# The last three expert weights loaded by column halves, and new step orders around them

## The chip, the cores and the metric

The kernel runs on one core of a Trainium2 chip. The metric is the device time of one execution in microseconds (us); lower is better. Times are medians of several executions, and the profile is one execution more.

## What is computed

Block-sparse attention feeds a soft mixture of experts. The reference, cut to what matters here:

```python
# attention: q, k, v are (4, 8, 768, 64); chunks of 32 keys, the best 6 chunks of each query are kept
ub = np.sum(np.maximum(q * k_min, q * k_max), axis=-1)          # bound of a chunk, causal
sel = the 6 chunks of largest ub;  mask = sel & causal
attn = softmax(where(mask, q @ k.T / 8, -1e9));  x = attn @ v   # then reshaped to (3072, 512)
# experts: phi (512, 32), w1 (8, 512, 1024), w2 (8, 1024, 512); 8 experts with 4 slots each
logits = x @ phi
d = softmax(logits, axis=0);  slot_input = d.T @ x              # over all 3072 rows
for e in range(8):
    slot_out[e] = relu(slot_input[e] @ w1[e]) @ w2[e]
c = softmax(logits, axis=1);  out = c @ slot_out                # (3072, 512), f32
```

All inputs and the output are float32 in DRAM. The kernel computes in bfloat16 with float32 sums.

## The kernel before

**Attention.** The 4 x 8 heads are taken as 16 pairs (0 to 15). An outer loop runs over i from -2 to 16, and in each round a string in the table `ORDER` (or `PLAIN`) names the steps to issue, one after the other. Every engine gets its instructions in that order, so the strings are the schedule: an engine that waits for one step holds up all that stands behind it in its own queue. Round i issues the scores (S0 to S5), the exponentials on ScalarE (E0 to E5) and the causal edges on GpSimd (A0 to A5) of pair i, the product with v of pair i-1 (P0 to P5), the bounds and the search for pair i+1 (UB, SL, SH, UN, NT, NC), the transposes of k and q for pair i+2 (KT, KE, KN, KX, QT, QE, QP, BD), and the normalising of pair i-2 (NO, XT, XE). Loads are steps too: LK, LQ, LV, W.

**The chain behind attention.** Rounds 13 to 15 also hold the expert softmax of the first three batches (MX, MT, MB, MS, MD, ME and RM, RS, RE). Round 16 is the chain behind the last pair: the last pair's product with v (ZPA, ZP3, ZP4, ZP5), normalising (ZN0, ZN1, ZN2), transposes and their copies (ZX0 to ZX2; Ze on ScalarE, ZE on VectorE), logits (ZL1, ZL3, ZL4), the maximum and its spreading (ZPM, ZPT, ZMB, ZLK, ZL2, ZSH, ZBC), the exponential (ZDX), the old batches' share of the slot inputs (D0 to D4, 18 matmuls each; DA copies the sum), the last batch's share (ZD0, ZD1), the sums (ZSA, ZS0, ZS1, ZSZ). Zk is a dummy matmul of 128 columns. Then the experts: `I{f}{g}` is the first product for hidden half f and expert group g, R0 and R1 the relu of half f, T0 and T1 the transposes of its result, `O{f}{g}{y}` the second product for output-column half y, O0 and O1 the slot outputs of half y.

**Output.** `H{m}.{y}` writes column half y of row group m (256 KB), `F{m}` a whole row group (512 KB). There are 12 groups; the first six are written by halves, all six left halves (y = 0) ahead of O011, O111 and O1, so ahead of any right half. The stores go through SyncE's queue.

**Weights.** All 16 weight matrices stay in SBUF as `w_sb[0..15]`: 0 to 7 are w1 and 8 to 15 are w2. Each is 2 MB in DRAM and is cast to 1 MB on the way by a DMA that GpSimd issues. Weights 0 to 11 have memory of their own. The last four take memory that attention gives up: number 12 in step CL (behind the last k and q), 13 in CU (behind the last bounds), 14 in ZCT (behind the last transposed k and q), 15 in ZCE (behind the last exponentials). `load_w` loads numbers 14 and 15 by column halves: the left half when the memory comes free, and both right halves in `close_e`, between the memory sets of two padded tiles (`siT`, `hT`) and of `zrow`. A half is two DMAs of 256 KB, one for each hidden half. The left half feeds the y = 0 products, the right half the y = 1 products.

Of the kernel before, what the change touches and what calls it, by code (L numbers as in the profile page):

```python
# [39 lines left out]
for _g, _pieces in enumerate(GROUPS):  # L40
# [11 lines left out]
LV A4 QP A5 BD""",  # L52
    1: """LV KT S0 LQ S1 LK UB E0 S2 E1 NO S3 P0 P1 A0 P2 SL KE SH E2 QT P3 A1 XT UN XE S4 W S5 KN E3 QE E4 E5
A5 P4 A2 KX A3 NT LG BD A4 NC P5 LC QP""",
    13: """S0 KT LV E0 S1 UB E1 A1 KE NO S2 S3 E2 E3 P0 P1 SL UN QT SH P2 QE P3 A3 A2 KN KX XT S4 S5 CL XE QP
E4 A0 W BD E5 P4 NT A5 LG P5 NC A4 LC MX""",
    14: """S0 E0 S1 UB S2 NO MT S3 RM P0 E1 E2 P1 E3 MB SL A1 A2 MS S4 MD A0 SH E4 UN P2 RS S5 XT P3 P4 A3 NT
NC E5 XE RE CU A4 A5 P5""",
    15: """NO S0 S1 C0 E0 S2 E1 P0 S3 E2 E3 V0 A1 XT P1 P2 A3 S4 A0 S5 P3 E4 A4 A2 E5 ME A5 P4 P5 XE""",
    16: """ZN0 ZPA ZP3 ZCT ZP4 D0 ZLH ZX0 ZN1 ZP5 Ze0 ZN2 D1 ZX1 ZL1 ZX2 D2 Ze1 ZL3 ZE2 ZL4 ZPM Zk ZPT ZMB D3  # L60
ZLK ZL2 ZSH ZBC D4 Zk ZCE ZDM ZDX DA ZD0 ZCI ZDE Zk ZSA ZS0 ZD1 ZS1 I00 I10 I01 I11 R0 ZRM R1 ZSZ
ZLC T0 C1 O000 V1 ZZ T1 O010 O100 O110 ZCX Zk Q0 O0 H0.0 O001 H1.0 Q1 H2.0 O101 H3.0 H4.0 H5.0 O011
O111 O1 H0.1 C2 V2 H1.1 Q2 F6 H2.1 F7 C3 v3 H3.1 F8 Q3 H4.1 F9 F10 H5.1 F11""",
}

# [2 lines left out]
def kernel(  # L68
# [16 lines left out]
    E, F = moe_w1.shape[0], moe_w1.shape[2]  # L85
# [4 lines left out]
    NO = OLD * NQT  # L90
# [50 lines left out]
    def load_w(i, ys=range(2)):  # L141

        if i < E:
            src = moe_w1[i].rearrange("(a p x) f -> p a (x f)", p=P, x=2)
            dst = w_sb[i].rearrange("p (a f) -> p a f", a=NDG // 2)
        else:
            src = moe_w2[i - E].rearrange("(a p x) d -> p a (x d)", p=P, x=4)
            dst = w_sb[i].rearrange("p (a f) -> p a f", a=NFG // 4)
        if i >= 2 * E - 2:
            src = moe_w2[i - E].rearrange("(a p x) (y d) -> y a p x d", p=P, x=4, y=2)  # L150
            dst = w_sb[i].rearrange("p (a x y d) -> y a p x d", a=NFG // 4, x=4, y=2)
            for y in ys:
                for a in range(2):
                    nc.gpsimd.dma_start(out=dst[y, a], in_=src[y, a])  # L154
        else:
            nc.gpsimd.dma_start(out=dst, in_=src)  # L156
# [41 lines left out]
    for n in "I K1 Q1 K2 Q2 W G M".split():  # L198
        if n[0] == "I":
            make_identity(nc, ident)  # L200
        elif n[0] == "W":
            load_w(0)
        elif n[0] == "V":
            load_v(int(n[1]))
        elif n == "G":
            nc.gpsimd.affine_select(
                out=qgrp, in_=qgrp, compare_op=ALU.not_equal, fill=1.0, base=0,
                pattern=[[-1, 4], [0, CH]], channel_multiplier=1,
            )
            nc.gpsimd.affine_select(  # L210
                out=caus[:4], in_=caus[:4], compare_op=ALU.is_ge, fill=NEG, base=0,
                pattern=[[0, 4], [-1, 4]], channel_multiplier=1,
            )
        elif n == "M":
            nc.gpsimd.affine_select(
                out=squad, in_=squad, compare_op=ALU.not_equal, fill=-NEG, base=0,
                pattern=[[-CH, 2], [-64, 2], [-1, NCHUNK]], channel_multiplier=1,
            )
            nc.gpsimd.affine_select(
                out=squad, in_=squad, compare_op=ALU.not_equal, fill=1.0, base=-NCHUNK,  # L220
                pattern=[[-CH, 2], [-64, 2], [0, NCHUNK]], channel_multiplier=1,
            )
        else:
            load(int(n[1]), n[0].lower())
# [319 lines left out]
    def weights(i):  # L544
        nonlocal nw
        for _ in range(wplan.get(i, 0)):
            load_w(nw)
            nw += 1

    def late_weight(*ys):  # L550
        n = len(w_sb)
        wt = ctx.enter_context(tc.tile_pool(name=f"wt{n}", bufs=1))
        w_sb.append(wt.tile([P, NFG * Dm], BF16, name=f"w_sb{n}"))
        load_w(n, *ys)
# [15 lines left out]

    def close_bounds(i):
        u_ctx.close()
        late_weight()

    def of(d, f, *a):
        return lambda i: f(i + d, *a) if have(i + d) else None
# [7 lines left out]
        "NO": of(-2, normalise), "XT": of(-2, x_transposes), "XE": of(-2, evac_x),  # L584
        "LG": lambda i: moe(moe_logits, i - 2), "LC": lambda i: moe(moe_copy, i - 2),
        "PHI": phi_load, "kc": lambda i: cast_first("k"), "qc": lambda i: cast_first("q"), "MASK": spread_mask, "CL": close_loads, "CU": close_bounds,
    }
    for g in range(len(GROUPS)):
# [23 lines left out]
    def close_e():  # L612
        e_ctx.close()
        late_weight([0])
        pads = ctx.enter_context(tc.tile_pool(name="pads", bufs=1))
        st["siT"] = pads.tile([P, NDG, E, CH], BF16, name="siT_pad")
        st["hT"] = pads.tile([P, NFG, E, CH], BF16, name="hT_pad")
        nc.gpsimd.memset(st["siT"], 0.0)
        load_w(2 * E - 2, [1])
        nc.gpsimd.memset(st["hT"], 0.0)  # L620
        st["tail"] = ctx.enter_context(tc.tile_pool(name="tail", bufs=1))
        st["zrow"] = st["tail"].tile([1, 4, CH], F32, name="zrow")
        nc.gpsimd.memset(st["zrow"], 1.0)
        load_w(2 * E - 1, [1])
# [94 lines left out]
    def slots_z():  # L719
# [8 lines left out]
    HX = range(NDG - 1)  # L728
    STEP.update({n: (lambda i, f=f, a=a: f(*a)) for n, f, *a in (
        ("ZCT", close_T), ("ZCE", close_e), ("ZCI", close_i), ("ZN0", normalise, LAST - 1),  # L730
        ("ZPA", pv, LAST, [0, 1, 2]), ("ZP3", pv, LAST, [3]), ("ZP4", pv, LAST, [4]), ("ZP5", pv, LAST, [5]),
        ("ZX0", x_transposes, LAST - 1), ("ZE0", evac_x, LAST - 1, 0, NQT, nc.vector.tensor_copy),
# [174 lines left out]
```

## Time and profile before

| | |
|---|---|
| median of 3 runs | 157.3 us (157.18 to 157.82) |
| the profiled execution's own time | 157.73 us |
| its span, first to last instruction | 155.8 us, mean granted TensorE clock 0.964 |
| busy: TensorE, VectorE, ScalarE, GpSimd | 87%, 75%, 79%, 63% of the span |
| read from DRAM, written to DRAM | 52.49 MB, 6.29 MB |

The profile gives busy time by engine and by stretch of time, the DMA engines' busy share and what they moved (counted on the SBUF side for a load, so a cast load of 200 GB/s reads 400 GB/s), groups of instructions by code line with what they waited for, and a chain of waits followed back from the last instruction. A busy share of the DMA engines above 1 means that more than one packet per engine was under way.

### The profile page before, as it was taken

The numbers are of one execution on the slowest core, as the hardware profiler recorded it, in microseconds if no ns is written. First come the engines' busy times: TensorE is split into PE (matmuls) and PEld (weight loads), VectorE is DVE, ScalarE is ACT, GpSimd is POOL, SyncE is SP. The second block draws the span as 40 slices with busy tenths as digits, with TensorE's granted clock in tenths as the row PEclk, the third lists the DMA queues.
The fourth block names the chain that finished last, engine by engine and source line by source line (L and its number), as shares of the span: only waits on it lengthen the run. The fifth ranks groups of instructions, "written<-read, shape, count | busy, mean of one in ns | idle before, by whom it ended". The sixth has DMA issues, their size and how long they took to land.

```text
span 155.8 us, 6234 instructions
## 1 busy us (share of the span) xinstructions
PE 135.7 (87%) x2591; PEld 95.5 (61%) x2591; DVE 117.0 (75%) x408; ACT 123.5 (79%) x165; POOL 98.3 (63%) x196
## 2 busy tenths in 40 slices
PE   6649899998999999999999999998999999877700
PEld 3335467766776777676767766685759856545400
DVE  5766979988889889898888989899946343439900
ACT  3669999999899999999989999998796303447900
POOL 7959895977789687796977885855627970000000
PEclk9956999999999999999999999999999999999995
DMA  4999999999999999999999999999999999998995
GB/s 161 176 207 199 168 220 183 193 216 186 213 194 206 201 184 212 196 208 200 182 208 200 207 202 200 207 203 192 200 215 211 214 198 194 159 325 306 392 404 219
DMA packets 46251, 33.32 MB, mean 214 GB/s; under 512 B 26512, under 2 KB 41872, under 8 KB 46224
## 3 DMA queue, kind: packets, MB, share of 16 engines
q0 software_dynamic: 41552, 25.86, 115.1%
q1 hardware_dynamic: 4672, 7.08, 12.4%
q8 instruction: 20, 0.33, 0.8%
q14 instruction: 7, 0.06, 0.1%
HBM read 52.49 MB, written 6.29 MB: 377 GB/s over the span
## 4 chain that ended last, share of the span: by engine, by line
POOL 26%; PE 20%; ACT 16%; DMA 14%; issue 10%; DVE 9%; POOLq 0%; ACTq 0%; DVEq 0%
ACT e_sb L365 10%; POOL e_sb L370 9%; DMA w_sb<-in_moe_w_dram 7%; DMA k_in<-in_k_dram 7%; POOL v_t L180 4%; PE at_ps L399 3%; PE sc_ps L342 3%; POOL q_in L163 3%; POOL w_sb L156 3%; POOL k_in L163 3%; ACT kT L249 2%; PE sc_ps L352 2%; PE tr_ps L240 2%; PE warm_ps L230 2%; POOL w_sb L154 2%
## 5 line engine op out<-in xcount | busy, mean ns | idle before, releaser
L365 ACT ACTIVATE e_sb<-sc_ps 128x768 bf16<-128x768 f32 (+1 forms) x96 | 83.0, 925 | 3.3 <-PE sc_ps L352 2.1
L370 POOL TENSOR_SCALAR_AFFINE_SELECT e_sb<-e_sb 128x256 bf16<-128x256 bf16 x96 | 37.1, 409 | 24.4 <-ACT e_sb L365 22.2
L342 PE MATMUL sc_ps<-qT,kT 64*128 64x384 bf16 (+3 forms) x288 | 39.9, 295 | 1.0 <-ACT e_sb L365 0.6
L352 PE MATMUL sc_ps<-nsT,smask 64*128 64x384 bf16 (+2 forms) x320 | 39.4, 278 | 0.0
L399 PE MATMUL at_ps<-v_t,e_sb 128*128 128x65 bf16 x672 | 27.7, 194 | 0.0
L399 PEld LDWEIGHTS <-e_sb 128*128 128x128 bf16 x672 | 23.9, 98 | 5.8 <-issue 5.3
L342 PEld LDWEIGHTS <-kT 64*128 64x128 bf16 x288 | 16.0, 94 | 10.0 <-issue 4.4
L352 PEld LDWEIGHTS <-smask 64*128 64x128 bf16 x320 | 17.4, 95 | 3.7 <-issue 0.4
L180 POOL DMA_DIRECT2D v_t<-in_v_dram x16 | 16.5, 1034 | 0.0
L412 DVE TENSOR_TENSOR x_sb<-at_ps,inv 128x768 bf16<-128x768 f32 (+1 forms) x17 | 15.5, 910 | 0.6
L259 DVE TENSOR_REDUCE mm<-kT 128x24 bf16<-128x768 bf16 x16 | 15.1, 943 | 0.1
L264 DVE TENSOR_REDUCE mm<-kT 128x24 bf16<-128x768 bf16 x16 | 15.1, 943 | 0.0
L249 ACT ACTIVATE qT<-tr_ps 128x768 bf16<-128x768 bf16 x16 | 13.0, 815 | 2.1 <-PE tr_ps L240 2.0
L307 DVE MAX8 mx_t<-ub_ps 128x8 f32<-128x16 f32 (+4 forms) x160 | 14.4, 163 | 0.0
L249 ACT ACTIVATE kT<-tr_ps 128x768 bf16<-128x768 bf16 x16 | 12.9, 805 | 0.7 <-PE tr_ps L240 0.7
L163 POOL DMA_DIRECT2D k_in<-in_k_dram x15 | 10.9, 726 | 0.8 <-issue 0.5
L163 POOL DMA_DIRECT2D q_in<-in_q_dram x15 | 10.8, 717 | 0.2 <-issue 0.2
L432 DVE COPY xT_sb<-xT_ps 128x768 bf16<-128x768 bf16 (+1 forms) x15 | 8.1, 543 | 2.8 <-PE xT_ps L421 1.6
L156 POOL DMA_DIRECT2D w_sb<-in_moe_w_dram x14 | 10.1, 718 | 0.0
L240 PE MATMUL tr_ps<-ident,k_in 128*64 128x128 bf16 x192 | 8.7, 229 | 1.5 <-DMA k_in<-in_k_dram 1.3
L240 PEld LDWEIGHTS <-k_in 128*64 128x64 bf16 x192 | 6.1, 113 | 5.9 <-DMA k_in<-in_k_dram 3.2
L240 PE MATMUL tr_ps<-ident,q_in 128*64 128x128 bf16 x192 | 9.0, 229 | 0.6 <-DVE q_in L174 0.4
(129 smaller groups left out, 215.3 us busy)
## 6 DMA issues: line engine op xcount, KB each, us to landing
w_sb<-in_moe_w_dram POOLq DMA_DIRECT2D x14, 1024.0 KB, 12.2
v_t<-in_v_dram POOLq DMA_DIRECT2D x16, 192.0 KB, 11.2
out_dram<-o_sb SPq DMA_DIRECT2D x12, 256.0 KB, 4.0
out_dram<-w_sb SPq DMA_DIRECT2D x6, 512.0 KB, 4.2
k_in<-in_k_dram POOLq DMA_DIRECT2D x15, 192.0 KB, 9.1
q_in<-in_q_dram POOLq DMA_DIRECT2D x15, 192.0 KB, 9.1
w_sb<-in_moe_w_dram POOLq DMA_DIRECT2D x8, 256.0 KB, 11.3
cT_all<-in_k_dram SPq DMA_DIRECT2D x1, 384.0 KB, 3.1
```

Source lines behind the costliest of these rows:

```text
L163: nc.gpsimd.dma_start(out=t, in_=src.rearrange("h (p g) d -> p h (g d)", p=P))
L180: nc.gpsimd.dma_start(out=v_t[i % NV][:, :, :, :D], in_=v[b, 2 * j:2 * j + 2].rearrange("h (g p) d -> p h g d", p=P),)
L240: nc.tensor.matmul(ps[h * 64:(h + 1) * 64, g, :], lhsT=src[:, h, g * D:(g + 1) * D], rhs=ident, is_transpose=True,)
L249: nc.scalar.activation(t.rearrange("d (p g) -> d p g", g=NQT), st.pop((nm + "ps", i)).rearrange("d g p -> d p g"), func=ACT.Copy, scale=-1 ...
L259: nc.vector.tensor_reduce(mm[:, 0, 0, :], kT, axis=AX.X, op=ALU.min, negate=True)
L264: nc.vector.tensor_reduce(st["mm", i][:, 1, 0, :], kT, axis=AX.X, op=ALU.max)
L342: nc.tensor.matmul(ps[:, h, c:c + w], lhsT=kT[r, kg * P:(kg + 1) * P], rhs=qT[r, qs], start=True, stop=False,)
L352: nc.tensor.matmul(ps[:, h, c + (f - t0) * P:c + (l - t0) * P], lhsT=smask[r, x, kg].rearrange("p a b -> p (a b)"), rhs=nsT[r, (f - x * NJ ...
L365: nc.scalar.activation(e[:, :, :w], st.pop(("scps", i, g))[:, :, :w], func=ACT.Exp, scale=-scale)
L370: nc.gpsimd.affine_select(out=e[:, :, :P], in_=e[:, :, :P], compare_op=ALU.is_ge, fill=0.0, base=0, pattern=[[0, 2], [1, P]], channel_mult ...
L399: nc.tensor.matmul(o, lhsT=st["e", i, g][:, h, c:c + P], rhs=v_t[i % NV][:, h, kg, :], start=(kg == 0), stop=(kg == t),)
L412: nc.vector.tensor_tensor(st["x", b][:, t0:t1, 2 * j:2 * j + 2, :].rearrange("p t h d -> p h t d"), at[:, :, :, :D], inv.broadcast_to([P, ...
```

## The change

Three things. Weight 13 joins 14 and 15 in being loaded by column halves: its left half is issued in CU, its right half in `close_e` ahead of the right half of 14. The strings for rounds 13, 14 and 15 are in a new order, with the same steps but two: the copy V0 moves from round 15 into round 16, and the exponential ME from round 15 into round 14. The string of round 16 is new too, up to O110; behind that it is as before. The order of the six left half groups and of all row groups behind them is the same in both kernels.

```diff
-    13: S0 KT LV E0 S1 UB E1 A1 KE NO S2 S3 E2 E3 P0 P1 SL UN QT SH P2 QE P3 A3 A2 KN KX XT S4 S5 CL XE QP
-        E4 A0 W BD E5 P4 NT A5 LG P5 NC A4 LC MX
+    13: S0 E0 S1 KT UB KE E1 LV S2 A1 QT E2 NO S3 P0 P1 SL CL QE KN P2 P3 E3 P4 UN KX P5 XT S4 XE A2 SH W S5
+        E4 E5 NT A3 LG QP A5 A0 NC A4 LC BD MX
-    14: S0 E0 S1 UB S2 NO MT S3 RM P0 E1 E2 P1 E3 MB SL A1 A2 MS S4 MD A0 SH E4 UN P2 RS S5 XT P3 P4 A3 NT
-        NC E5 XE RE CU A4 A5 P5
+    14: S0 E0 S1 S2 UB NO MT E1 MB S3 P0 P1 A0 E2 SL A1 P2 RM A2 E3 MS SH S4 S5 P3 E4 MD UN P4 A4 E5 P5 A3
+        NT RS ME XT A5 NC XE CU RE
-    15: NO S0 S1 C0 E0 S2 E1 P0 S3 E2 E3 V0 A1 XT P1 P2 A3 S4 A0 S5 P3 E4 A4 A2 E5 ME A5 P4 P5 XE
+    15: S0 S1 C0 NO S2 P0 E0 E1 P1 E2 XT S3 S4 A2 E3 A0 A3 P2 P3 E4 P4 A1 XE S5 P5 E5 A4 A5
-    16: ZN0 ZPA ZP3 ZCT ZP4 D0 ZLH ZX0 ZN1 ZP5 Ze0 ZN2 D1 ZX1 ZL1 ZX2 D2 Ze1 ZL3 ZE2 ZL4 ZPM Zk ZPT ZMB D3
-        ZLK ZL2 ZSH ZBC D4 Zk ZCE ZDM ZDX DA ZD0 ZCI ZDE Zk ZSA ZS0 ZD1 ZS1 I00 I10 I01 I11 R0 ZRM R1 ZSZ
-        ZLC T0 C1 O000 V1 ZZ T1 O010 O100 O110 ZCX Zk Q0 O0 H0.0 ...
+    16: D0 ZPA ZP3 Zk V0 ZN0 ZP4 ZX0 ZLH Ze0 ZN1 ZP5 ZN2 ZCT D1 ZX1 ZL1 ZX2 D2 ZE1 ZE2 ZL3 ZL4 D3 ZPM ZLK
+        ZPT ZMB ZL2 ZSH ZBC ZDM ZCE D4 ZDX DA ZCI ZD0 ZDE ZSA ZS0 ZD1 ZS1 I00 I01 I10 R0 ZRM I11 R1 ZSZ T0
+        C1 O000 V1 ZZ T1 O010 O100 O110 ZLC ZCX Zk Q0 O0 H0.0 ...

 def load_w(i, ys=range(2)):
-        if i >= 2 * E - 2:
+        if i >= 2 * E - 3:

 def close_bounds(i):
         u_ctx.close()
-        late_weight()
+        late_weight([0])

 def close_e():
         nc.gpsimd.memset(st["siT"], 0.0)
+        load_w(2 * E - 3, [1])
         load_w(2 * E - 2, [1])
         nc.gpsimd.memset(st["hT"], 0.0)
```

More of the change, by code (lines that the diff above doesn't have):

```diff
@@ L54 @@
 A5 P4 A2 KX A3 NT LG BD A4 NC P5 LC QP""",
[L55 to L60, printed above, removed]
-ZLK ZL2 ZSH ZBC D4 Zk ZCE ZDM ZDX DA ZD0 ZCI ZDE Zk ZSA ZS0 ZD1 ZS1 I00 I10 I01 I11 R0 ZRM R1 ZSZ
-ZLC T0 C1 O000 V1 ZZ T1 O010 O100 O110 ZCX Zk Q0 O0 H0.0 O001 H1.0 Q1 H2.0 O101 H3.0 H4.0 H5.0 O011
+    13: """S0 E0 S1 KT UB KE E1 LV S2 A1 QT E2 NO S3 P0 P1 SL CL QE KN P2 P3 E3 P4 UN KX P5 XT S4 XE A2 SH W S5
+E4 E5 NT A3 LG QP A5 A0 NC A4 LC BD MX""",
+    14: """S0 E0 S1 S2 UB NO MT E1 MB S3 P0 P1 A0 E2 SL A1 P2 RM A2 E3 MS SH S4 S5 P3 E4 MD UN P4 A4 E5 P5 A3
+NT RS ME XT A5 NC XE CU RE""",
+    15: """S0 S1 C0 NO S2 P0 E0 E1 P1 E2 XT S3 S4 A2 E3 A0 A3 P2 P3 E4 P4 A1 XE S5 P5 E5 A4 A5""",
+    16: """D0 ZPA ZP3 Zk V0 ZN0 ZP4 ZX0 ZLH Ze0 ZN1 ZP5 ZN2 ZCT D1 ZX1 ZL1 ZX2 D2 ZE1 ZE2 ZL3 ZL4 D3 ZPM ZLK
+ZPT ZMB ZL2 ZSH ZBC ZDM ZCE D4 ZDX DA ZCI ZD0 ZDE ZSA ZS0 ZD1 ZS1 I00 I01 I10 R0 ZRM I11 R1 ZSZ T0
+C1 O000 V1 ZZ T1 O010 O100 O110 ZLC ZCX Zk Q0 O0 H0.0 O001 H1.0 Q1 H2.0 O101 H3.0 H4.0 H5.0 O011
 O111 O1 H0.1 C2 V2 H1.1 Q2 F6 H2.1 F7 C3 v3 H3.1 F8 Q3 H4.1 F9 F10 H5.1 F11""",
```

## The prediction, made before the change was run

> **What bounds the kernel now.** I read the page first: the engine shares, the DMA row, the queues and the bytes.
>
> ```profile
> span 155.8 us, 6234 instructions
> DMA  4999999999999999999999999999999999998995
> GB/s 161 176 207 199 168 220 183 193 216 186 213 194 206 201 184 212 196 208 200 182 208 200 207 202 200 207 203 192 200 215 211 214 198 194 159 325 306 392 404 219
> HBM read 52.49 MB, written 6.29 MB: 377 GB/s over the span
> ```
>
> No compute engine is above 87%, but the DMA engines are at nine tenths or more from the second slice to nearly the end. For 34 slices they load (about 200 GB/s on the SBUF side, so 400 read), then they store at about 400. A reordering of compute can gain only where that stream has a hole or where its tail is badly used. So next came the chain of waits over the last third, in order of time (start, length, what), and the DMA rows by issue (the lines on landing stand under the issue that they belong to):
>
> ```profile
> 127.74 10.80 DMA w_sb<-in_moe_w_dram
> 138.58 0.61 PE so_ps L810 x13
> 139.22 0.48 ACT so_sb L817
> 139.74 0.28 PE o_ps L840
> 140.05 0.48 DVE o_sb L847
> ```
> ```profile
> L156 POOL DMA_DIRECT2D w_sb<-in_moe_w_dram x1: 716/716/716, 104.9 to 104.9; - x1
> DMA to landing us min/median/max: 17.2/17.2/17.2
> ```
> ```profile
> L156 POOL DMA_DIRECT2D w_sb<-in_moe_w_dram x1: 722/722/722, 110.7 to 110.7; - x1
> DMA to landing us min/median/max: 16.7/16.7/16.7
> ```
> ```profile
> L154 POOL DMA_DIRECT2D w_sb<-in_moe_w_dram x2: 742/742/742, 120.4 to 121.2; - x2
> DMA to landing us min/median/max: 11.3/11.6/11.9
> ```
> ```profile
> L853 SPq DMA_DIRECT2D out_dram<-o_sb x1: 612/612/612, 135.2 to 135.2; - x1
> ```
> ```profile
> L853 SPq DMA_DIRECT2D out_dram<-o_sb x1: 534/534/534, 140.7 to 140.7; - x1
> ```
>
> Weight 11 lands at 104.9 + 17.2 = 122.1, weight 13 (whole) at 110.7 + 16.7 = 127.4, the left half of 15 at 121.2 + 11.9 = 133.1, the last right half at 127.74 + 10.80 = 138.54. From a landing to the first store of that half it is 135.2 - 133.1 = 2.1 us on the left and 140.7 - 138.54 = 2.2 us on the right. Then the stretches of one microsecond (length; busy time of PE, PEld, DVE, ACT, POOL with instructions; clock, DMA share, GB/s), and the two DMA queues from 136.0 to 136.5 and from 136.5 to 137.0 (packets, MB, share); q0 holds the loads, q1 the stores:
>
> ```profile
> 133.00:134.00 1.00, 0.89 (x20) 0.61 (x20) 0.00 (x0) 0.28 (x1) 0.00 (x0) 1.00 1.44 195
> 135.00:136.00 1.00, 1.00 (x26) 0.67 (x22) 0.61 (x4) 0.60 (x3) 0.00 (x0) 1.00 0.89 114
> 141.00:142.00 1.00, 0.89 (x13) 0.83 (x14) 0.90 (x4) 0.28 (x2) 0.00 (x0) 1.00 0.47 164
> 150.00:151.00 1.00, 0.00 (x0) 0.00 (x0) 0.00 (x0) 0.00 (x0) 0.00 (x0) 1.00 1.04 422
> ```
> ```profile
> q0 software_dynamic: 94, 0.05, 69.5%
> q1 hardware_dynamic: 4, 0.00, 2.4%
> ```
> ```profile
> q1 hardware_dynamic: 101, 0.10, 61.0%
> q0 software_dynamic: 78, 0.04, 57.0%
> ```
>
> Three things are to be seen. **One:** the load stream falls from 195 to 114 GB/s before the stores move (4 packets before 136.5, 101 in the half microsecond behind it, so they begin 1.3 us behind their first issue). The drop says that some of the 16 DMA engines have finished all loads near 134.5 to 135 and others drag on. Landing needs the slowest. **Two:** from 136.5 stores and remaining loads share the slow engines, 101 packets against 78. **Three:** the left stores run out, and from 141 to 142 the share is 0.47; the right half's stores then fill the engines to the end, which compute no longer touches (150 to 151: no engine busy, share 1.04). So the end is set by the landing of the last right half: 2.2 us of compute, then 18 units of 256 KB (six right halves, six whole groups at two each), and the span ends 155.8 - 140.7 = 15.1 us behind the first right store's issue. Whatever moves the landing moves the end by as much.
>
> **The change part by part.** The sum is made on the profiled execution: 157.73 us, span 155.8, so 1.9 us lie around the span. It is 0.4 us over the median of 157.3; I carry the difference over to the median.
>
> *Weight 13 by halves, bytes.* The same 2 MB are read, in shorter pieces. Four DMAs of halves, the left of 14 and 15, landed between 127.4 and 133.1: 5.6 us per MB written; the whole weight 13 took 127.4 - 122.1 = 5.4. By rate it is more:
>
> ```profile
> 114.00:118.00 4.00, 3.87 (x84) 2.94 (x83) 0.89 (x3) 3.95 (x6) 2.09 (x6) 1.00 1.06 214
> 127.00:134.00 7.00, 6.70 (x135) 4.12 (x128) 1.30 (x6) 1.82 (x5) 0.74 (x1) 1.00 1.45 196
> ```
>
> 1.05 MB at 214 GB/s is 4.9 us, at 196 5.35, so +0.45. I take +0.3 us for the load stream, with 0.2 and 0.5 as ends (the rates are from long stretches, the landings nearer to the place).
>
> The Trainium skill (DMA: Bandwidth & Descriptors, Specifications) gives 512 B as the least piece for line rate, and the pieces here are just that (0.05 MB in 94 packets). By that rule this term would be nought and the sum 0.6 us lower, 158.1; the rows have the halves slower, and I go by them (the rule's time lies in the forecast's low end, and has its chance there).
>
> *Left halves earlier.* The right half of 13 (two DMAs, at 5.6 / 4 = 1.4 us each) goes behind the three left halves, so the last left half lands 2.8 - 0.1 = 2.7 us earlier, near 130.4. That alone gives little, as the chain of compute arrives at the same time. These are the rows of the timeline (start, length, engine, line, count) on which the chain's terms rest:
>
> ```profile
> 117.67 0.69 ACT L484 ACTIVATE d_o<-ld 128x576 bf16<-128x576 f32 x1
> 118.52 0.60 PE L509 MATMUL h_ps<-d_o,x_sb 128*128 128x32 bf16 x18
> 119.40 0.55 PE L399 MATMUL at_ps<-v_t,e_sb 128*128 128x65 bf16 x12
> 122.46 0.60 PE L509 MATMUL h_ps<-d_o,x_sb 128*128 128x32 bf16 x18
> 124.56 0.22 PE L639 MATMUL h_ps<-w_sb,ident 128*128 128x128 bf16 x1
> 125.94 3.64 PE L770 MATMUL h_ps<-w_sb,siT_pad 128*32 128x512 bf16 x64
> 128.91 1.32 ACT L777 ACTIVATE h_sb<-h_ps 128x512 bf16<-128x512 f32 x2 [4.27 <-PE h_ps L770]
> 133.09 0.60 PE L810 MATMUL so_ps<-w_sb,hT_pad 128*32 128x256 bf16 x13 [0.24 <-DMA w_sb<-in_moe_w_dram]
> ```
>
> The last matmuls of the left half waited 0.24 us for a weight. So the weight's gain of 2.7 us is cut to 0.24 unless the chain gets shorter too.
>
> *The chain's new order.* D0 (118.52, 18 matmuls) stood between ZP4 and ZP5 on PE's queue; now it goes ahead of ZPA, where PE waits for ScalarE anyway. It needs ME's result, and ME moves to round 14, so that is ready. Gain up to 0.4 at ZP5 (119.40), on which ZN2, the last transposes and the last logits hang. D3 (122.46) stood between ZPT and ZL2; ahead of ZPM it lies under the maximum on VectorE: 0.2 to 0.4. Two dummies Zk (124.56, 0.22 each) around ZD0 and ZD1 go: 0.2. Now I00 and I01, both groups of hidden half 0, come first, so R0 starts after half of the 3.64 us and not after three quarters, and T0 is held only by PE's end of I11: before, R0 ran from 128.9 to 129.5 while PE's products ended at 129.58; 0.1 at most. The copy ZE1 moves to VectorE between ZN2 and ZE2, under ZX2 on PE: nothing; ZLC and ZCX move behind O110, and C3 that needs them comes long after: nothing. On the other side ME (0.69) now runs on ScalarE in round 14, ahead of the exponentials of pair 15, which are back to back until 117.67; ScalarE waited 0.71 us ahead of E4 of pair 14 (its row stands below), and the new order has S4 and S5 earlier, so I take that cover as enough: nothing, or 0.7 later where it fails. With the 0.24 the terms add to about 1.1; parts of them overlap (PE runs in order and waits for other engines in between), so I take 0.8 us, with -0.5 (the chain later) and 1.3 as ends. The first left store then moves from 135.2 to 134.4, its bytes from 136.5 to 135.7.
>
> ```profile
> 109.98 1.72 ACT L365 ACTIVATE e_sb<-sc_ps 128x768 bf16<-128x768 f32 x2 [0.71 <-POOL ns_t L311]
> 127.74 0.74 POOL L154 DMA_DIRECT2D w_sb<-in_moe_w_dram  x1 [0.86 <-DMA w_sb<-in_moe_w_dram]
> ```
>
> *What the earlier stores collide with.* On the slow engines, loads that are left when stores begin get about half of the engine (78 packets of 179 above). Before: from 136.5 to 138.54 is 2.04 us, so 1.0 us of undisturbed loading was left, and the stream alone would have ended at 137.5. After: alone 137.5 + 0.3 = 137.8; stores from 135.7; 2.1 us of loading left, doubled 4.2, so the last right half lands at 139.9: 1.36 us later. The six left halves keep the queue filled that long: 0.26 MB at 404 GB/s (the last full slice of the page) is 0.65 us each, 3.9 us together, above 2.1. What the earlier start fills on the fast engines is paid back as a longer hole: left stores run out near 141.5 as before, and the first right bytes move at 139.9 + 2.2 + 1.3 = 143.4.
>
> *Added waits on POOL.* Four more DMA issues at 0.74 us, two of them in `close_e` ahead of hT's memory set. In the row at 127.74 the last issue waited for an earlier weight, and the only one to land then is 13, eight DMAs before it. With the same distance of eight the right half of 14 would wait for the left of 13 (near 124.9), that of 15 for the left of 14 (near 127.7), with two memory sets queued behind. Issues end near 129, some 7 us ahead of their turn in the stream: nothing, unless POOL falls far behind.
>
> Rounds 13 to 15 move GpSimd's weight issues by a microsecond or two, against 13 to 17 us from issue to landing, so the stream stays filled: nothing.
>
> Sum: +1.36, rounded 1.4: 157.73 becomes 159.1 profiled, 157.3 becomes **158.7 us**.
>
> **The rivals.** *Halves' cost only.* The chain isn't shorter in the end, stores start at 136.5: 137.8 - 136.5 = 1.3, doubled 2.6, landing 139.1, +0.6: 157.9. For it: each term of the chain is a few tenths, and ME sits on ScalarE.
>
> *Faster: the engines drain together.* The drag may come from how the last four DMAs follow one another, not from slow engines. Then with six right DMAs queued in one go all engines finish together: from 134.5 on about 0.31 MB were loaded (114 GB/s for 2 us is 0.23, 0.04 in the row from 136.5, and as much again, an estimate, behind that), 1.6 us at 196, plus 0.3: 136.4. With stores from 135.7 the last 0.7 doubles: landing 137.1, -1.4, 155.9 (0.7 us of loads and 3.9 us of left stores from 135.7 end at 140.3, just ahead of the right bytes at 140.6, so the tail follows). It decides if the share stays at 1.4 until the loads end. Against it: the drop is sudden, as if a group of engines was done.
>
> *The chain gets later.* If ME and RE hold up pair 15 by the full 0.7, stores start at 137.2, 0.6 of load is left, doubled 1.2, landing 138.4: 157.2, no change.
>
> *POOL late.* If the waits of eight add up and the last right DMA is issued after 131, with 8 us or more from issue to landing under sharing, it lands past 140.5: +2, 159.3 or more.
>
> **How the numbers follow.** About 0.5% (0.8 us) is what a measurement of this kernel can tell from no change. Forecast 0.52; halves' cost only 0.17; engines together 0.14; chain later 0.10; POOL late 0.07. The forecast's own ends: chain 1.3 and bytes 0.5 give 2 x (138.0 - 135.2) = 5.6, landing 140.8, +2.3; the low end meets the first rival. The range 156.6 to 159.6 leaves out most of the faster case and the far upper end. Faster by over 0.5% is the third case, 0.14. Within 0.5%: the fourth, most of the halves' case and the foot of the forecast, 0.27. Slower: 0.59.
>
> **What would show it.** Right: the last left half lands near 130.4 and no PE wait on it is left; first store issued near 134.4; the last right half lands at 139 to 140.5; the hole behind the left stores is 1.5 us or more where it was under 1; from the first right store to the span's end it is 15.1 us as before. Wrong: a last landing at or before 138.5; a DMA share that stays near 1.4 to the last load; a first left store at or after 135.2; a hole in the load stream between 105 and 130; or another time than 15.1 us from the first right store to the end.

## The result, and the profile after

The changed kernel takes 158.62 us in the median of 21 runs (157.74 to 159.91), the kernel before 157.56 in the same comparison (157.11 to 158.76, 21 runs). The ratio is 1.0056 with a 95% interval of 1.0039 to 1.0073: slower by 0.9 us (0.6 to 1.2), where 1.4 was forecast; the two medians lie 1.1 apart. In this text a few executions that the chip disturbed are left out of the ratios, not of the medians. The profiled execution of the changed kernel took 158.25 us (157.73 before), so it shows 0.5 of the 0.9; where the rest comes from is found below.

The page and the chain of waits of the changed kernel, the same lines as were shown for the kernel before:

```profile
span 156.2 us, 6234 instructions
DMA  4999999999999999999999999999999999997995
GB/s 157 168 211 201 168 218 186 194 214 186 214 193 211 199 182 212 194 212 196 182 207 199 205 203 198 208 204 188 204 215 204 196 198 194 200 340 254 392 405 221
...
129.23 9.74 DMA w_sb<-in_moe_w_dram
139.01 0.61 PE so_ps L811 x13
```

The last right half lands at 129.23 + 9.74 = 138.97, 0.43 us later than the 138.54 before, and the span is 0.4 longer. The DMA row has one new digit, a 7 (eight tenths before) in the slice behind the one with the landing: a longer hole. SyncE's issues (start, length, how many) and the first store of a right half:

```profile
134.64 7.83 SPq L854 DMA_DIRECT2D out_dram<-o_sb  x8
...
L854 SPq DMA_DIRECT2D out_dram<-o_sb x1: 533/533/533, 141.1 to 141.1; - x1
```

The first left store comes at 134.64 and not 135.2, the first right one at 141.1 and not 140.7. From there to the span's end it is 156.2 - 141.1 = 15.1 us, as before. The stretches of one microsecond around the tail of the changed kernel, and then the two of the kernel before that were not shown (the columns are those of the prediction):

```profile
134.00:135.00 1.00, 1.00 (x26) 0.76 (x26) 0.61 (x2) 0.51 (x2) 0.00 (x0) 1.00 1.47 206
135.00:136.00 1.00, 1.00 (x23) 0.56 (x20) 0.80 (x3) 0.81 (x2) 0.00 (x0) 1.00 1.15 158
140.00:141.00 1.00, 0.83 (x10) 0.62 (x9) 0.52 (x2) 0.53 (x2) 0.00 (x0) 1.00 0.80 277
141.00:142.00 1.00, 0.56 (x10) 0.44 (x10) 0.99 (x3) 0.54 (x2) 0.00 (x0) 1.00 0.38 125
142.00:143.00 1.00, 0.74 (x7) 0.51 (x6) 0.91 (x3) 0.66 (x2) 0.00 (x0) 1.00 0.79 266
```
```profile
140.00:141.00 1.00, 0.67 (x10) 0.39 (x7) 0.95 (x3) 0.77 (x2) 0.00 (x0) 1.00 1.03 344
142.00:143.00 1.00, 0.66 (x8) 0.45 (x7) 1.00 (x3) 0.96 (x2) 0.00 (x0) 1.00 0.96 326
```

Behind the left stores 1.0 us of DMA time is missing from a share of 1 in the changed kernel (0.20 + 0.62 + 0.21), 0.6 before (0.53 + 0.04). Left stores start earlier and end earlier, the right ones start later.

### The profile page after: what moved, and what is told of

Same layout as the page of the kernel before. It is cut to its first block, busy times and chain, and to the rows that moved or that the text cites. A ratio compares the mean times of both kernels' runs of the same rounds, so it can differ in the third digit from the quotient of the medians.

```text
span 156.2 us, 6234 instructions
## 1 busy us (share of the span) xinstructions
PE 135.4 (87%) x2589; PEld 95.7 (61%) x2589; DVE 116.8 (75%) x409; ACT 123.3 (79%) x164; POOL 100.4 (64%) x199
## 4 chain that ended last, share of the span: by engine, by line
ACT 25%; DMA 24%; POOL 16%; PE 16%; issue 9%; DVE 4%; SPq 0%; ACTq 0%; POOLq 0%
ACT e_sb L365 19%; DMA w_sb<-in_moe_w_dram 14%; DMA k_in<-in_k_dram 7%; POOL e_sb L370 6%; PE sc_ps L342 4%; ACT kT L249 3%; DMA cT_all<-in_q_dram 3%; PE sc_ps L352 2%; PE tr_ps L240 2%; PE at_ps L399 2%; POOL w_sb L156 2%; POOL v_t L180 2%; POOL q_in L163 2%; ACT w_sb L850 2%; POOL w_sb L154 1%
## 5 line engine op out<-in xcount | busy, mean ns | idle before, releaser
L399 PE MATMUL at_ps<-v_t,e_sb 128*128 128x65 bf16 x672 | 27.1, 194 | 0.0
L352 PEld LDWEIGHTS <-smask 64*128 64x128 bf16 x320 | 17.3, 95 | 3.5 <-issue 0.4
L264 DVE TENSOR_REDUCE mm<-kT 128x24 bf16<-128x768 bf16 x16 | 15.1, 943 | 0.0
L259 DVE TENSOR_REDUCE mm<-kT 128x24 bf16<-128x768 bf16 x16 | 15.1, 942 | 0.0
L156 POOL DMA_DIRECT2D w_sb<-in_moe_w_dram x13 | 9.3, 718 | 0.2 <-issue 0.2
```

The source lines that it names most:

```text
L259: nc.vector.tensor_reduce(mm[:, 0, 0, :], kT, axis=AX.X, op=ALU.min, negate=True)
L264: nc.vector.tensor_reduce(st["mm", i][:, 1, 0, :], kT, axis=AX.X, op=ALU.max)
L352: nc.tensor.matmul(ps[:, h, c + (f - t0) * P:c + (l - t0) * P], lhsT=smask[r, x, kg].rearrange("p a b -> p (a b)"), rhs=nsT[r, (f - x * NJ ...
L399: nc.tensor.matmul(o, lhsT=st["e", i, g][:, h, c:c + P], rhs=v_t[i % NV][:, h, kg, :], start=(kg == 0), stop=(kg == t),)
```

## The experiments

**What each part does alone.** The first two kernels carry one part of the change each, the next two take the left stores away from in front of the right halves.

Halves only: the kernel before, with

```diff
-        if i >= 2 * E - 2:
+        if i >= 2 * E - 3:
 def close_bounds(i):
-        late_weight()
+        late_weight([0])
 def close_e():
+        load_w(2 * E - 3, [1])
         load_w(2 * E - 2, [1])
```

> The kernel before with weight 13 by column halves alone; every order as before. Sharing theory (the prediction's: loads that are left when the stores begin get half of the slow DMA engines): the 0.24 us wait for the last left half goes, first left store near 135.0, last right half lands at 138.9 to 139.3 (138.54 before), time +0.4 to +0.8 us. Own-pace rival (the slow engines load one half of 256 KB per 1.3 us whatever the stores do, and only the shorter pieces count): last right half at 138.9, time +0.4. Rival that the new orders carry the loss: no change, within 0.2 us.

Measured: 158.19 us against 157.69, ratio 1.002 (0.9989 to 1.0051), first left store at 134.79, last right half at 129.48 + 9.78 = 139.26. Its profiled execution, 159.2 us, was the longest of its 12; why is seen below. The landing is where the sharing theory put it and 0.36 past the own-pace figure of 138.9, and the interval of the time contains no change, so this run does not decide between the two.

Orders only: the changed kernel with those edits taken back.

> The changed kernel's orders for rounds 13 to 16 with weight 13 loaded whole, as before. Sharing theory: the chain is ready early but the last left half lands at 133.1 as before, so first left store 135.0 to 135.2, last right half 138.5, time within 0.3 us of before. Own-pace rival: the same. Rival that the new orders carry the loss: +0.5 us or more.

Measured: 157.79 against 157.69, ratio 1.0005 (0.9971 to 1.0039); last right half at 127.38 + 10.8 = 138.2, 0.3 earlier than forecast, and the first left store at 136.29, a microsecond later than forecast (this profile, 158.82 us, is one of the long executions explained below). No loss is seen from the orders. The landing moved later with the halves and not with the orders (over all profiles by 0.5, below), so the halves are what delays it; the two intervals of time alone would not separate the parts.

No left stores, of before and of after: `H0.0` to `H5.0` and `H0.1` to `H5.1` become `F0` to `F5`, all behind `O1`.

> The kernel before with no store ahead of the right halves: all twelve row groups are written whole, behind O1, so that the weights' last loads run alone. Sharing theory: the last right half lands at 137.5, 1.0 us earlier than the 138.54 with six left stores beside it; span near 158.7. Own-pace rival: it lands at 138.4 to 138.6 all the same; span near 159.7.

> The changed kernel with no store ahead of the right halves, all twelve row groups whole behind O1. Sharing theory: the last right half lands at 137.8 (138.97 with the left stores beside it). Own-pace rival: 138.8 to 139.1, and 0.4 later than in the same edit of the kernel before, which is the price of the shorter pieces alone.

Measured: 160.82 and 161.18 us, one run each; the span of the first is 159.1, between the two forecasts. The chains of waits, the first of the edit of before, the second of the edit of after:

```profile
127.28 10.78 DMA w_sb<-in_moe_w_dram
```
```profile
129.35 9.22 DMA w_sb<-in_moe_w_dram
```

Landing at 138.06 and 138.57: 0.5 and 0.4 earlier than with the left stores, not 1.0 and 1.2, and not unchanged either as the own-pace rival had it. But with no store in the way the changed kernel still lands 0.5 later than the kernel before, which in this pair is the price of the pieces and the orders without any store. And the 0.5 and 0.4 are no effect of the stores. The left half of 15, which lands before any store moves, was 0.7 earlier in the first (132.4 against 133.1) and 0.5 in the second (130.4 against 130.9): these executions' streams were ahead as a whole. The packets of the two queues say it directly. From 136 to 137 and from 137 to 138, the changed kernel with its stores running (q0 loads, q1 stores):

```profile
q0 software_dynamic: 214, 0.11, 80.2%
q1 hardware_dynamic: 162, 0.16, 48.0%
...
q1 hardware_dynamic: 256, 0.25, 73.9%
q0 software_dynamic: 117, 0.06, 42.4%
```

and the same two stretches of the changed kernel without left stores:

```profile
q0 software_dynamic: 213, 0.10, 81.0%
...
q0 software_dynamic: 139, 0.07, 51.5%
```

With 162 store packets beside them 214 load packets went through, without them 213. In the second stretch it is 117 against 139, which could be a small price of the stores. The changed kernel run once more (below) answers it: in that execution the stores did not move before 138.2, and its two stretches hold no store packets at all:

```profile
q0 software_dynamic: 209, 0.10, 77.2%
...
q0 software_dynamic: 114, 0.05, 42.0%
```

Its last right half landed at 138.9, as with stores from 135.9 on. The sharing step falls. The own-pace rival stands: the slow DMA engines load one half per 1.3 us, whether stores run or not. In the changed kernel's rows the halves landed at 133.6, 135.0, 136.3, 137.6 and 139.0, with stores beside the last two and the end of the third.

The trace also shows why. It records sixteen completions of each DMA, which are taken here as one for each of the 16 engines. Those of the last right half come at 135.6 to 136.2 (seven of them) and at 137.1 to 139.0 (nine). Those of the first left store come at 137.0 to 137.2 (seven) and at 137.8 to 139.7 (nine), and rank by rank the last nine are 0.68 to 0.72 us behind the load's nine. So an engine that had loads left finished them first, and the stores that ran beside loads ran on engines that were done. The records do not name the engines, so that the ranks belong to the same engines is a reading, but it holds in the kernel before too (0.68 to 0.75 us for the last seven).

**What the pieces cost.** Three stretches of the kernel before, then the same of the changed one:

```profile
113.00:119.00 6.00, 5.68 (x127) 4.35 (x124) 2.85 (x6) 5.31 (x7) 3.01 (x7) 1.00 1.07 215
119.00:126.00 7.00, 6.54 (x172) 5.86 (x171) 3.55 (x14) 2.16 (x5) 6.43 (x9) 1.00 1.10 209
126.00:133.00 7.00, 6.81 (x131) 4.00 (x132) 2.17 (x12) 1.54 (x4) 1.62 (x4) 1.00 1.43 195
```
```profile
113.00:119.00 6.00, 5.80 (x126) 4.29 (x122) 3.03 (x7) 5.31 (x7) 3.34 (x8) 1.00 1.07 216
119.00:126.00 7.00, 6.62 (x174) 5.96 (x170) 4.00 (x15) 1.68 (x4) 6.25 (x10) 1.00 1.35 195
126.00:133.00 7.00, 6.92 (x144) 4.31 (x144) 2.35 (x13) 1.65 (x4) 3.97 (x5) 1.00 1.45 197
```

The stream runs at 215 GB/s while whole weights pass and at 195 to 197 in pieces of 512 B, with more packets under way (share 1.4 against 1.1). The changed kernel enters the slow regime one weight earlier. In the stretch from 119 to 126 it loads 14 GB/s less for 7 us, 0.10 MB, which takes 0.5 us at 195. That is the size of the landing's delay. Every profile shows the rate: in this stretch the nine with weight 13 in halves and 12 whole load at 194 to 197 GB/s, the four with 13 whole at 208 or 209, under old orders and new. The last landings of the nine average 138.94 and those of the four 138.44, 0.5 us between the means. Single profiles overlap (138.57 to 139.48 against 138.06 to 139.02), so one pair of profiles could not have shown it.

Four weights in halves: weight 12 too, left half in CL, right half first in `close_e`.

> The changed kernel with weight 12 by column halves as well (left half in CL, right half first in the row of right halves), so four weights in halves. The prediction's sharing step has fallen by now (loads keep their pace beside stores), so the loss should be the price of the shorter pieces: own-pace theory, one more weight in pieces lands the last right half 0.4 to 0.7 us later than the changed kernel, 139.4 to 139.6, and the time is 0.4 to 0.7 us above the changed kernel's. Rival that pieces are free and the landing moved for another reason (the orders, the later issues): no more than 0.2 us above the changed kernel.

Measured: 159.83 us over six executions, ratio 1.0106 (1.0068 to 1.0145), so 0.75 us over the changed kernel by the ratios (1.3 by the medians); landing at 130.96 + 9.25 = 140.2. Time and landing are both past the upper ends of 0.7 and 139.6 that the piece theory gave, and the run tests more than pieces: from 119 to 126 its stream falls to 160 GB/s.

```profile
119.00:126.00 7.00, 7.00 (x195) 6.47 (x191) 4.23 (x12) 1.94 (x5) 6.32 (x9) 1.00 1.22 160
```

The left half of 14 is issued at 119.8 and lands 4.7 us later (10.4 before), so the queue ran short: a left half puts only half a weight into the stream until ZCE frees the right ones. In the changed kernel the same issue took 7.8 us and the stream kept 195. This run says that another half costs more, not that pieces alone do it.

**The spread.**

> The changed kernel as it is, beside the other runs of this call. Own-pace theory and sharing theory alike: 0.4 to 0.7% over the kernel before; last right half at 138.9 to 139.3; span minus that landing 17.3 us as before.

Measured: 158.55 against 157.66, ratio 1.0058 (1.0029 to 1.0086); landing 138.9. But its profiled execution (159.44 us, span 157.4) has its first left store 2.3 us later than the other, at 136.9, and 18.5 us from the landing to the end instead of 17.3. The stretches show the granted clock (second figure from the right but one) at half speed in the first expert product:

```profile
126.00:127.00 1.00, 0.58 (x16) 0.32 (x16) 0.87 (x6) 0.00 (x0) 1.00 (x2) 0.78 1.45 197
127.00:128.00 1.00, 1.00 (x16) 0.37 (x12) 0.20 (x1) 0.00 (x0) 1.00 (x1) 0.50 1.46 197
128.00:129.00 1.00, 1.00 (x16) 0.44 (x12) 0.24 (x2) 0.00 (x0) 1.00 (x3) 0.50 1.45 195
129.00:130.00 1.00, 1.00 (x16) 0.33 (x8) 0.00 (x0) 0.00 (x0) 0.87 (x2) 0.51 1.42 201
```

The orders-only kernel shows the same from 125.9 to 129.3. In the halves-only profile it is at the other end, in the wake of TensorE's two waits of 0.7 us for the last right halves (waits of 0.6 and 0.7 are there in the changed kernel's first profile too, without a drop):

```profile
141.00:142.00 1.00, 1.00 (x8) 0.52 (x5) 0.65 (x2) 0.45 (x1) 0.00 (x0) 0.50 0.33 108
142.00:143.00 1.00, 0.77 (x11) 0.59 (x10) 0.76 (x3) 0.47 (x1) 0.00 (x0) 0.50 0.47 163
143.00:144.00 1.00, 1.00 (x6) 0.75 (x5) 0.97 (x2) 0.54 (x1) 0.00 (x0) 0.50 0.63 215
```

The clock is low from 140.6 to 144.0, the right half's chain runs at half speed, and the hole behind the left stores grows to 4 us at a DMA share of 0.33 to 0.63. Each of these drops lasts 3.4 us. The Trainium skill (TensorE: Matmul & The Clock Gate, Part 1: The HAM clock gate) says that the clock is set from activity in free-running windows of 3.4 us, and the drops' length agrees; by that rule it depends on where the windows fall in an execution whether a thin stretch is punished. The clock records of the traces fit that: within an execution all changes lie whole multiples of 3.41 us apart (17.34, 126.56, 129.97 and 150.45 in the profile above). The times fit too: of the changed kernel's 33 executions 32 count in the ratio of their run; the ten of them with a mean granted clock of 0.948 or less took 158.6 to 159.9 us, with a median of 159.3, and the other 22 have a median of 158.3. The sorting is not clean, as an execution that starts at full clock can have the drop and a higher mean (0.967 in the profile above). Two cures were tried. Dummies back: `D4 ZDX` to `D4 Zk ZDX`, `ZDE ZSA` to `ZDE Zk ZSA`.

> The changed kernel with the two dummy matmuls Zk of 128 columns back at their old places around ZD0 and ZD1. Clock theory (without them TensorE idles 0.4 us ahead of I00, and in some executions, as in the profile of the second run of the changed kernel, its granted clock falls to 0.5 from 126 to 130, so the first left store comes at 136.9): the profile shows clock 1.00 from 122 to 134, idle ahead of I00 under 0.25 us, first left store near 134.7, and the median falls by 0.2 to 0.6 us from the changed kernel's, to a ratio of 1.002 to 1.0045. Rival that the pieces of weight 13 are the whole loss: ratio 1.005 to 1.007 as before.

Measured: 158.64 against 157.66, ratio 1.0066 (1.0041 to 1.0092), the profile at clock 1.00 between 122 and 134, the first left store at 134.5. No gain; the two dummies' removal is not what lets the clock fall, and the run with nine left groups, which has them too, shows the drop at 126 (its 64 products take 5.32 us instead of 3.64) with no idle time ahead of them. Dummies in the right half's waits, besides:

```diff
+    def fill(i):
+        ps = st["p_tp"].tile([P, 512], F32, name="fill_ps", tag="tp")
+        for _ in range(3):
+            nc.tensor.matmul(ps, lhsT=ident, rhs=w_sb[0][:, :512], start=True, stop=True)
-    H5.0 O011 O111
+    H5.0 FL O011 FL O111
```

> As the run with the dummies back, and six more dummy matmuls of 512 columns, three ahead of O011 and three ahead of O111, where TensorE waits 0.6 to 0.7 us for the last right halves. Clock theory: the drop to 0.5 at 141 to 144, seen in the profiles of the halves-only and the four-weights kernels, goes too; fewer long executions, ratio 1.001 to 1.004, at or below the run with the dummies back. Pieces-only rival: 1.005 to 1.007; if the dummies hold up the right half, up to 0.4 us more.

Measured: 158.24 against 157.66, ratio 1.003 (1.0011 to 1.0049). All 11 executions lie between 157.91 and 158.53, and none has a mean clock below 0.955; of the 11 with the two dummies alone seven are above 158.53. So here the fill took the long executions away, and what is left of the loss is 0.5 us (0.2 to 0.8), the size of the landing's delay. The two intervals still meet (1.0039 to 1.0049); the split of 0.9 into 0.5 and 0.4 is a reading of medians and spread, not separated by the ratios alone. Nor is the fill a sure cure: the last run below has dummies ahead of the right half too, and two of its 12 executions took 158.96 and 159.38.

**The hole.** Eight left groups in front instead of six, in both kernels: `T1` becomes `C2 T1 V2`, `Q2` goes ahead of `H5.0`, `O011 O111` becomes `O011 H6.0 H7.0 O111`, and `F6`, `F7` become `H6.1`, `H7.1` near the end.

> The kernel before with eight left half groups in front of the right ones instead of six (the combine weights of the third batch, C2, V2 and Q2, move up to make this possible; they cost about 0.2 us in front of the first left store). Own-pace theory: stores take nothing from the loads, so the last right half still lands at 138.3 to 138.8, and the hole behind the left stores (141 to 142, DMA share 0.47) is filled: span minus landing falls from 17.3 to 16.4 to 16.8, time 0.5 to 0.9 us under before. Sharing theory: more stores beside the last loads delay the landing past 139, and the time is within 0.3 us of before.

Measured: 157.87 against 157.66, ratio 1.0012 (0.9993 to 1.0031): a miss, and both the time and the landing (139.02) are where the sharing theory had them. But the delay is not the stores': right halves landed at 134.3, 136.8, 137.7 and 139.0, so the slip lies between the first two, where the steps are 1.3 in the changed kernel, and store packets began only at 136.6. One packet of the instruction queue lies in that stretch (134 to 136, the share is that of 16 engines over 2 us), 16 KB long and busy for about 1 us:

```profile
q8 instruction: 1, 0.02, 3.0%
```

If it held up one slow engine, that engine's later loads came later by up to its length; the trace doesn't name the engine, so this stays a reading. The kernel before has such a packet at 134.4, and its halves slipped there too, by less (134.4, 136.4). The hole is only half filled, as the first right store comes at 141.8 and not at 140.7: 0.5 of that is the landing, and 0.6 is the two added groups, which stand ahead of O1 on PE and ScalarE (2.8 us from the landing to the store, 2.2 before).

```profile
141.00:142.00 1.00, 0.97 (x12) 0.75 (x11) 1.00 (x4) 0.99 (x3) 0.00 (x0) 1.00 0.63 219
```

> The changed kernel with eight left half groups in front (same edit). Own-pace theory: the landing stays at 138.9 to 139.2, the hole of 141 to 142.6 shrinks to less than 0.5 us, time 0.6 to 1.0 us under the changed kernel, so near or below before. Sharing theory: landing past 139.5 and no gain over the changed kernel.

Measured: 157.88 against 157.66, ratio 1.0014 (0.9989 to 1.0039), so 0.7 us under the changed kernel (1.0058), as forecast. The first right store stays (141.0), the landing too (138.8), and the share in the hole rises from 0.38 to 0.84:

```profile
141.00:142.00 1.00, 1.00 (x11) 0.69 (x10) 1.00 (x3) 0.99 (x3) 0.00 (x0) 1.00 0.84 295
```

So the later landing costs only as far as no left store is left to fill the wait. With eight left groups in both kernels the change makes no difference that shows (1.0012 and 1.0014). Nine left groups with the dummies back, and eight with dummies at all waits (one of 512 columns behind ZBC, two behind ZD1, three ahead of O011, one ahead of O111):

> The changed kernel with the dummies back and nine left half groups in front. Hole theory: nine left stores last from 136 to about 142, the first right bytes come at 142.4, so the DMA share stays at or above 0.9 from 137 to the end; span minus the last landing under 16.7 us; the median is 0.3 to 0.8 us under the kernel before (ratio 0.995 to 0.998). Rival that something else sets the end by then (issue on SyncE's queue, or the landing delayed by the stores): ratio 0.999 to 1.003.

> The changed kernel with both cures: eight left half groups in front, and dummy matmuls of 512 columns where TensorE waits (one behind ZBC, two behind ZD1, three ahead of O011, one ahead of O111). If the hole (0.7 us, from the run with eight left groups) and the clock drops in some executions (0.3 us of the median, from the run with six dummies) add, the median is 0.9 to 1.1 us under the changed kernel's, ratio to before 0.997 to 1.001, and the long executions above 158.6 are gone. Rival that the two are one effect (a drop hurts only where there is a hole to widen): ratio 1.001 to 1.003. If the dummies ahead of I00 don't prevent the drop at 126, the profile or the spread still shows it.

Measured: nine groups 158.27, ratio 1.004 (1.0014 to 1.0066), above both forecasts; the profile had the drop at 126, the first left store at 136.55 and a share of 0.52 from 142 to 143, so the nine stores came late and still left a hole. Eight with dummies 157.78 against 157.7, ratio 1.001 (0.9986 to 1.0034), within the interval of eight without, and on the border between its two forecasts. The cures were not seen to add. Why is open: the longer of the two long executions named above has a mean clock of 0.947, which suggests that these dummies did not keep the clock up every time. No version here beats the kernel before.

## Why the prediction was right, and where its working was wrong

**What bounds the kernel: right.** The end follows the last landing. It is 17.3 us from the one to the other in both profiles, and 15.1 us from the first right store. Where the clock had fallen it is more (18.5 in the second run of the changed kernel), as the left stores then came late.

**Pieces, +0.3: right in kind, too small.** 0.4 us in the profile pair, 0.5 by the rate, 0.5 over all profiles; the upper end of 0.5 from the rates was the better reading than the landings. The Trainium skill's 512 B (DMA: Bandwidth & Descriptors, Specifications) as enough for line rate isn't borne out for these casting loads: 195 against 215 GB/s.

**Left half 2.7 us earlier: it landed at 130.9, 2.1 earlier, and no PE wait on it is left.** The first left store came 0.6 earlier, inside the range around 0.8, but not from the chain's terms. I00 starts at 126.04 (125.94 before). The exponentials of pair 15 in the kernel before, and then rows of ScalarE and PE in the changed one, show why:

```profile
112.57 5.22 ACT L365 ACTIVATE e_sb<-sc_ps 128x768 bf16<-128x768 f32 x6 [0.20 <-PE sc_ps L352]
```
```profile
111.81 0.68 ACT L484 ACTIVATE d_o<-ld 128x576 bf16<-128x576 f32 x1
113.04 2.52 ACT L365 ACTIVATE e_sb<-sc_ps 128x768 bf16<-128x768 f32 x3
115.78 2.81 ACT L365 ACTIVATE e_sb<-sc_ps 128x1024 bf16<-128x1024 f32 x3 [0.21 <-PE sc_ps L352]
...
131.60 1.50 PE L811 MATMUL so_ps<-w_sb,hT_pad 128*32 128x256 bf16 x48
```

The exponentials of pair 15 end at 118.6 where they ended at 117.8. They start 0.5 later, behind ME, and lose 0.3 more on the way (0.21 of it in a wait for scores). So the cover taken for ME failed for the most part, and as I00 starts no earlier, what moving D0 and D3 and dropping the dummies gave was eaten up by it; no run separates these terms. The 0.6 is the weight's own: the 48 products of the left half run through from 131.60 to 133.10, where 13 of them had waited until 133.09 and ended at 133.69. A wait of 0.24 us in a PE row is its idle time behind modelled ends, not what the wait costs.

**Sharing, 1.1 of the 1.4: wrong.** The step "loads that are left when stores begin get about half of the engine" failed. 44% of the packets going to loads doesn't mean that loads lost anything: 214 and 117 packets beside stores, 209 and 114 without. The 44% was a share over all engines; engine by engine the stores came behind the loads. The landing was forecast at 139.9 and came at 138.97. The longer hole was forecast at 1.5 us or more and is 1.0.

**POOL's waits: right, nothing.** The last issue ends at 130.0, 9 us ahead of its landing, and the halves land evenly.

**What the working lacked:** executions in which the granted clock falls. By the run with the fill they bring the loss from 0.5 to 0.9 us, so the total came nearer to the forecast than its steps deserve. That the median of 158.62 lies so close to 158.7 is luck: 1.1 of the forecast 1.4 did not happen, and a cause that the working did not have made up for part of it. The rival of the halves' cost only came nearer in the landing (139.1), though it rested on the same sharing step.

## What to carry to other kernels

A transfer that is split to let its first part arrive sooner can be paid for by the whole stream (0.5 us for one weight here); before splitting, compare the stream's rate in both piece sizes and ask whether the consumer was waiting for the part at all. Where loads drain into stores, the end is set by the last landing plus what follows it, unless enough stores are ready to fill the wait. Two queues in one row of packets aren't proof of contention: count the packets of the one with the other taken away, and look at when each engine finishes.

## What the runs showed of the hardware

Stores beside loads took nothing that shows from the loads' rate (214 and 117 load packets in two microseconds with stores, 209 and 114 without, the same kernel), and the first store's completions lay 0.7 us behind the last load's on the engines that finished late. The engines ended 3.4 us apart in the changed kernel's first profile (the completions of the last right half run from 135.6 to 139.0). The Trainium skill (DMA: Bandwidth & Descriptors, Latency and other measured facts) names two engines that tend to be slower with software-issued transfers. In that profile nine of the sixteen completions come at least 0.9 us behind the other seven, so more than two lag; which they are and why stays open.

A weight in pieces of 512 B was loaded at 195 GB/s with a share of 1.4, whole at 215 with 1.1. Whether the 512 B written or the 1 KB read makes the difference wasn't tried.

The granted clock fell to 0.5 for 3.4 us in some executions of one and the same kernel and not in others, and dummy work in the waits ahead of the right half's products took the long executions away in one kernel (157.91 to 158.53 over 11 executions) and not in another (up to 159.38). Why the new orders let it fall at 126 even with no idle time ahead isn't settled.
